# Top-k attention with a capacity-limited expert layer: the order of one maximum, one pick and one mask in every second step

## The chip, the cores and the metric

The kernel runs on one core of a Trainium2 chip. A core has five engines that run side by side, each with its own stream of instructions, and wait for one another through semaphores: TensorE (PE in the profile, with its weight loads as PEld), VectorE (DVE), ScalarE (ACT), GpSimd (POOL) and SyncE (SP), which here only issues transfers. The metric is the device time of one execution in microseconds (us).

## What is computed

Two blocks follow each other. The first is attention over 8 batches, 8 heads, 576 positions and 64 features, in which each row keeps its 32 largest scores and drops the others:

```python
scores = scale * np.matmul(q, k.transpose(0, 1, 3, 2))
kth = np.partition(scores, -top_k, axis=-1)[..., -top_k:-top_k + 1]
mask = scores >= kth
scores = np.where(mask, scores, -1000000000.0)
...
attn = np.exp(scores)
attn = attn / (np.sum(attn, axis=-1, keepdims=True) + 1e-09)
return np.matmul(attn, v).astype(np.float32)
```

The second takes the 4608 x 512 result as tokens, sends each to the best of 8 experts, keeps the 80 tokens with the largest gate per expert, and runs two matrix products with a ReLU between them on those:

```python
logits = x @ w_gate
expert_idx = np.argmax(logits, axis=1)
...
h = np.maximum(x[tok_idx] @ w1[e], 0.0)
out[tok_idx] = gate_w[tok_idx, None] * (h @ w2[e])
```

All of the change lies in the first block: in how the 32nd largest score of each row is found, and in the mask that is made from it.

## The kernel before

The work is cut into 288 **units**. Two heads make a head pair; there are 32 head pairs, n = 0 to 31. A head pair has four full row tiles of 128 rows with two heads each, which are eight units, and one last tile in which the remaining 64 rows of both heads stand below one another, which is the ninth unit. So unit u = 9n + o, with o = 0 to 8, and a unit is a matrix `s` of 128 rows and 576 scores.

The threshold of a unit is found in this way (`search`, cuts marked). The eight largest of each of six parts (`parts`, not shown) are candidates; three rounds of maximum and replacement on the 48 candidates give the 24th largest of these, `w9[:, 7]`. ScalarE counts, with a sign function, how many scores lie above it. A product of the scores with that sign turns the larger ones negative, so that the maximum over the product gives the next eight scores below. The pick then takes from those nine values the one that the count calls for: the 32nd largest.

```python
def search(self, i):
    ...
            nc.scalar.activation(sign, s, Act.Sign, bias=w9[:, 7:8], scale=-1.0, accum_out=cnt)      # L266
    ...
    y = self.rows.tile([P, S], F32, name="y", tag="y", bufs=1)
    engine = nc.gpsimd if i in self.odd else nc.vector
    engine.tensor_tensor(out=y, in0=s, in1=sign, op=Alu.mult)                                        # L273, the product
    yield
    nc.vector.max(out=w9[:, 8:], in_=y)                                                              # L275, the maximum
    yield
    pick = self.small.tile([P, TOP_K - G0 + 1], F32, name="pick", tag="pick")
    nc.vector.scalar_tensor_tensor(out=pick, in0=past, scalar=cnt, in1=w9[:, 7:], accum_out=self.thr[:, i : i + 1],
                                   op0=Alu.is_equal, op1=Alu.mult)                                   # L278, the pick
    yield
```

The product of an odd unit is made by GpSimd, that of an even one by VectorE; there is one buffer `y` for both. The mask of dropped scores is made the other way round, by ScalarE for odd units and by GpSimd for even ones:

```python
def below(self, i):
    self.top.pop(i)
    mask = self.mask_of(i)
    if i in self.odd:
        nc.scalar.activation(mask, self.s[i], Act.Relu, bias=self.thr[:, i : i + 1], scale=-1.0)     # L294
        return
    nc.gpsimd.tensor_scalar(mask, self.s[i], self.thr[:, i : i + 1], None, op0=Alu.is_lt)            # L296
```

TensorE transposes the scores of a tile into PSUM (L334), adds the mask times a huge negative number (L340), ScalarE takes the exponential (L343 and L344), and TensorE multiplies by `v` (L357). A tile has one or two units, and its mask product in TensorE's stream comes behind the masks of both.

The units are pipelined by hand. A loop over steps emits, in step i, pieces of the units i to i - 4. The letters of a string give the order: each stands for one piece, and `lag` says of which unit.

```python
lag = dict(a=0, b=1, c=1, d=1, e=1, y=2, g=3, h=4, m=4)

for c in "ghmGbGycGdGGGeaz" if i % 2 else "GbGhmgcGdGeGGyaz":
    if c == "G":
        if 0 <= i < NU:
            next(first[i])                 # one of the six parts' maxima, L250
    elif c == "a":
        ...                                # the last part, then the first round on the candidates, L261
    elif c == "z":
        for u in drawn:
            self.over(*u)                  # reciprocal of the row sums, L369
    elif c == "m":
        if 0 <= i - lag[c] < NU:
            self.below(i - lag[c])         # the mask
    elif i - lag[c] in second:
        next(second[i - lag[c]])           # b, c, d, e: rounds; y: product; g: maximum; h: pick
...
if whole(i - 4):
    self.turn_w(*units[i - 4][:2], gate)   # transposes, mask products, exponentials of the tile
...
```

So in an even step, `y` is VectorE's product of unit i - 2, `g` is the maximum over GpSimd's product of the odd unit i - 3 (issued to GpSimd in the step before), `h` is the pick of the even unit i - 4, and `m` is GpSimd's mask of that unit. Instructions run on each engine in the order in which they are emitted.

Of the kernel before, what the change touches and what calls it, by code (L numbers as in the profile page):

```python
# [27 lines left out]
def kernel(  # L28
# [120 lines left out]
    class Attention:  # L149
# [299 lines left out]
        def run(self, slow):  # L449
# [13 lines left out]
            def whole(i):  # L463

                return 0 <= i < NU and units[i][2] > 0

            def step(i, last):
                if 0 <= i < NU:
                    n, t, h = units[i]
                    if t == 2 and h == 1 and n + 2 < NP:  # L470
                        self.load(n + 2, *divmod(n + 2, HP))
                    if t == 3 and h == 1 and n + 2 < NP:
                        self.load_v(n + 2, *divmod(n + 2, HP))
                    if t in (1, 3) and h == 0 and slow and n:
                        slow.pop(0)()
                    if t == 0 and h == 0 and n + 1 < NP:
                        due.append(n + 1)
                    first[i] = self.parts(i)

                lag = dict(a=0, b=1, c=1, d=1, e=1, y=2, g=3, h=4, m=4)  # L480

                for c in "ghmGbGycGdGGGeaz" if i % 2 else "GbGhmgcGdGeGGyaz":
                    if c == "G":
                        if 0 <= i < NU:
                            next(first[i])
                    elif c == "a":
                        if 0 <= i < NU:
                            next(first[i], None)
                            second[i] = self.search(i)
                            next(second[i])  # L490
                    elif c == "z":
                        for u in drawn:
                            self.over(*u)
                    elif c == "m":
                        if 0 <= i - lag[c] < NU:
                            self.below(i - lag[c])
                    elif i - lag[c] in second:
                        next(second[i - lag[c]])
                done = list(drawn)
                drawn.clear()  # L500

                def back():
                    if whole(i - 5):
                        self.back(*units[i - 5][:2])
                        drawn.append(units[i - 5][:2])


                rest = whole(i - 4) and units[i - 4][2] == 2
                if rest:
                    back()  # L510
                def gate():
                    for g in later:
                        if ready[g] == 2:
                            ready[g] = next(g)

                if whole(i - 4):
                    self.turn_w(*units[i - 4][:2], gate)
                for u in done:
                    self.divide(*u)

                ends = [(n, range(NK) if n < NP - 1 else range(NF) if t < NF else range(NF, NK))
                        for n, t in done if t == NF or (n == NP - 1 and t == NF - 1)]

                f = i + 4 if i not in (0, 1) else i + 3
                busy = 0 <= f < NU and units[f][2] != 1
                if busy:
                    self.front(*units[f][:2])
                if not rest:
                    back()
                if due and not busy and i > 0:  # L530
                    self.turn(due.pop())
                    busy = True
                for g in list(later):
                    if (ready[g] == 1 and busy or ready[g] == 2 and i < NU + 4) and not last:
                        continue
                    busy = busy or ready[g] == 1
                    ready[g] = next(g, None)
                    if ready[g] is None:
                        later.remove(g)
                for n, cs in ends:  # L540
                    b, hp = divmod(n, HP)
                    later.append(self.norm(n, b, hp, b % 2, 2, cs))
                    ready[later[-1]] = 0

            with tc.manual_schedule():
                for n in range(2):
                    self.load(n, *divmod(n, HP))
                    self.load_v(n, *divmod(n, HP))
                nc.sync.dma_start(wg, moe_w_gate.rearrange("(c p) e -> p c e", p=P))
                self.turn(0)  # L550
                i = -4
                while i < NU + 6 or later:
                    step(i, i >= NU + 5)
                    i += 1
# [391 lines left out]
```

## Time and profile before

| | |
|---|---|
| time, median of 3 runs | 989.52 us (988.08 to 991.57) |
| profiled execution | span 986.1 us, 35265 instructions |
| DVE, chain that ended last | 59% of the span |
| PE, chain that ended last | 29% of the span |
| the maximum (L275), 288 times | 752 ns each on DVE |
| the pick (L278), 288 times | 230 ns each on DVE |
| the product (L273), 144 times each | 740 ns on DVE, 1281 ns on GpSimd |
| the mask, 144 times each | 785 ns on ACT (L294), 1722 ns on GpSimd (L296) |
| the sign (L266), 288 times | 781 ns each on ACT |

The attention loop takes most of the span, from about 12 us to about 850 us; then routing and the experts follow. A line of the profile's timeline gives start and duration in us, the engine, the line of the kernel, the operation, what is written from what is read, the shapes, and in brackets how long the engine was idle just before it and what ended that. VectorE's instructions overlap a little at their ends: the time from one start to the next is shorter than the duration that is shown. An instruction with an accumulated output (the sign, the pick) is followed by a short read of the accumulator, and only then is its result there.

### The profile page before, as it was taken

To read this page: it belongs to the slowest core of one execution; us is meant where nothing else is said; L and a number is where in the kernel's file an instruction comes from. 1 tells how busy PE (TensorE), PEld (TensorE's weight loads), DVE (VectorE), ACT (ScalarE), POOL (GpSimd) and SP (SyncE) were. 2 spreads that over 40 slices of the span, in tenths; PEclk is the share of its full clock that TensorE was granted. 3 is DMA by queue.
4 is the path that set the end of the run, shared out by engine and by line. 5 is a ranking of instruction groups with operands and counts; after the bars stand their busy time and mean duration, and the time that the engine had idled before them with its cause. 6 is when DMAs were issued, how large, how long until landed. Compare 5 with 4: busy or idle time off the path is not lost.

```text
span 986.1 us, 35265 instructions
## 1 busy us (share of the span) xinstructions
PE 865.1 (88%) x13112; PEld 679.3 (69%) x13112; DVE 866.3 (88%) x5072; ACT 786.7 (80%) x1652; POOL 451.9 (46%) x333
## 2 busy tenths in 40 slices
PE   5898989898898998998889898988898898699896
PEld 3676767676666776776667676666676776578896
DVE  5999999999999999999999999999999999561110
ACT  4899999999899999999999999998999998501110
POOL 2455545555455555454555555554555555201111
PEclk9999999999999999999999999999999999979999
DMA  3445453333333333332221222222222200085910
GB/s 86 111 131 139 133 141 100 100 99 99 80 95 99 88 93 99 99 99 68 57 57 48 52 50 53 57 57 57 57 57 56 55 17 14 17 338 180 375 52 25
DMA packets 189812, 90.99 MB, mean 92 GB/s; under 512 B 139712, under 2 KB 176576, under 8 KB 189632
## 3 DMA queue, kind: packets, MB, share of 16 engines
q1 hardware_dynamic: 188608, 86.03, 31.5%
q0 software_dynamic: 1024, 2.62, 0.9%
q8 instruction: 105, 1.72, 0.7%
q14 instruction: 75, 0.61, 0.2%
HBM read 68.44 MB, written 20.19 MB: 90 GB/s over the span
## 4 chain that ended last, share of the span: by engine, by line
DVE 59%; PE 29%; ACT 7%; issue 3%; POOL 1%; DMA 1%; SPq 0%; POOLq 0%; ACTq 0%; DVEq 0%
DVE cand L250 19%; DVE w L275 14%; DVE cand L269 7%; DVE y L273 7%; PE cc L357 6%; PE sp L234 4%; DVE top L261 4%; PE yp L830 4%; PE sp L209 4%; DVE pick L278 3%; DVE w L261 2%; PE ab L334 2%; ACT wT L344 2%; ACT mask L294 1%; PE ab L340 1%
## 5 line engine op out<-in xcount | busy, mean ns | idle before, releaser
L250 DVE MAX8 cand<-s 128x8 f32<-128x96 f32 x1728 | 389.6, 246 | 9.1 <-ACT s L242 8.9
L296 POOL TENSOR_SCALAR mask<-s,thr_all 128x576 bf16<-128x576 f32 x144 | 247.9, 1722 | 149.6 <-DVE pick L278 130.1
L273 POOL TENSOR_TENSOR y<-s,sign 128x576 f32<-128x576 f32 x144 | 184.5, 1281 | 261.8 <-DVE pick L278 121.9
L266 ACT ACTIVATE sign<-s,w 128x576 bf16<-128x576 f32 x288 | 224.9, 781 | 29.6 <-DVE w L261 27.3
L357 PEld LDWEIGHTS cc<-vb,wT 128*64 128x64 f32 x5760 | 182.1, 138 | 92.0 <-ACT wT L344 90.7
L357 PE MATMUL cc<-vb,wT 128*64 128x65 f32 x5760 | 204.4, 225 | 25.7 <-ACT wT L344 25.7
L275 DVE MAX8 w<-y 128x8 f32<-128x576 f32 x288 | 216.6, 752 | 1.3 <-POOL y L273 1.3
L234 PE MATMUL sp<-both 64*128 64x288 f32 (+1 forms) x1280 | 202.0, 435 | 5.7 <-ACT s L242 3.8
L242 ACT ACTIVATE s<-sp 128x1152 f32<-128x1152 f32 (+1 forms) x161 | 167.6, 1042 | 10.5 <-PE sp L234 9.8
L334 PE MATMUL ab<-ident,s 128*128 128x128 f32 x1148 | 175.9, 281 | 0.0
L344 ACT ACTIVATE wT<-ab 128x1024 f32<-128x1024 f32 (+1 forms) x159 | 149.6, 941 | 5.6 <-PE ab L340 4.1
L234 PEld LDWEIGHTS sp<-both 64*128 64x128 f32 (+1 forms) x1280 | 105.5, 179 | 45.2 <-ACT s L242 6.2
L334 PEld LDWEIGHTS ab<-ident,s 128*128 128x128 f32 x1148 | 127.2, 141 | 11.7 <-issue 0.9
L340 PEld LDWEIGHTS <-mask 128*128 128x128 bf16 x1312 | 76.9, 97 | 79.1 <-issue 37.3
L261 DVE MAX8 top<-cand 128x8 f32<-128x48 f32 x576 | 115.2, 200 | 0.0
L294 ACT ACTIVATE mask<-s,thr_all 128x576 bf16<-128x576 f32 x144 | 113.0, 785 | 0.5
L269 DVE MATCH_REPLACE8 cand<-top,cand 128x48 f32<-128x48 f32 x576 | 111.0, 193 | 0.1
L273 DVE TENSOR_TENSOR y<-s,sign 128x576 f32<-128x576 f32 x144 | 106.6, 740 | 0.8 <-ACT sign L266 0.8
L340 PE MATMUL ab<-huge,mask 128*128 128x128 bf16 x1148 | 89.9, 219 | 0.0
L340 PE MATMUL cc<-huge,mask 128*128 128x128 bf16 x160 | 35.7, 223 | 58.9 <-ACT mask L294 29.0
L380 ACT ACTIVATE xn<-cc,z_all 128x64 f32<-128x64 f32 (+1 forms) x320 | 85.8, 315 | 1.2 <-DVE z_all L369 0.8
L278 DVE SCALAR_TENSOR_TENSOR pick<-past,cnt,w 128x9 f32<-128x9 f32 x288 | 66.4, 230 | 0.2 <-DVE z_all L369 0.2
(187 smaller groups left out, 856.0 us busy)
## 6 DMA issues: line engine op xcount, KB each, us to landing
w<-in_moe_w_dram SPq DMA_DIRECT2D x10, 2048.0 KB, 16.0
vb<-in_v_dram SPq DMA_DIRECT2D x96, 128.0 KB, 2.7
w<-in_moe_w_dram SPq DMA_DIRECT2D x24, 512.0 KB, 3.8
out_dram<-zero SPq DMA_DIRECT2D x9, 1024.0 KB, 5.8
qn<-in_q_dram SPq DMA_DIRECT2D x64, 128.0 KB, 2.3
kn<-in_k_dram SPq DMA_DIRECT2D x64, 128.0 KB, 2.6
xd<-xn SPq DMA_DIRECT2D x32, 256.0 KB, 2.2
qn<-in_q_dram SPq DMA_DIRECT2D x32, 32.0 KB, 2.5
```

Source lines behind the costliest of these rows:

```text
L234: nc.tensor.matmul(o, lhsT=qT[d, t * P : t * P + m], rhs=kT[d, j * HS : (j + 1) * HS], start=True, stop=True)
L250: nc.vector.max(out=cand[:, j, :], in_=s[:, j * S // NG : (j + 1) * S // NG])
L261: nc.vector.max(out=dst, in_=cand)
L266: nc.scalar.activation(sign, s, Act.Sign, bias=w9[:, 7:8], scale=-1.0, accum_out=cnt)
L269: nc.vector.match_replace(out=cand, in_to_replace=dst, in_values=cand, imm_value=LOW)
L273: engine.tensor_tensor(out=y, in0=s, in1=sign, op=Alu.mult)
L275: nc.vector.max(out=w9[:, 8:], in_=y)
L296: nc.gpsimd.tensor_scalar(mask, self.s[i], self.thr[:, i : i + 1], None, op0=Alu.is_lt)
L334: nc.tensor.matmul(o, lhsT=sc[:, keys[c]], rhs=ident, start=c in (0, NF, NF + 1), stop=False, is_transpose=True, skip_group_check=True)
L340: nc.tensor.matmul(dst[c], lhsT=mk[:, keys[c]], rhs=minus if self.lean else huge, start=False, stop=True, skip_group_check=True)
L344: nc.scalar.activation(wT[:, : g * NF, :], ab.rearrange("p h c r -> p (h c) r")[:, : g * NF, :], Act.Exp, scale=scale / TINY)
L357: nc.tensor.matmul(cc[r : r + TL, o], lhsT=wT[:, h * NF + c if c < NF else 2 * NF, r : r + TL], rhs=vb[:, k, :], start=(c == 0), stop=(c = ...
```

## The change

In even steps the maximum over GpSimd's product (`g`) is emitted ahead of the pick (`h`) and of GpSimd's mask (`m`). Odd steps stay as they are; there the maximum has always come first.

```diff
                 lag = dict(a=0, b=1, c=1, d=1, e=1, y=2, g=3, h=4, m=4)

-                for c in "ghmGbGycGdGGGeaz" if i % 2 else "GbGhmgcGdGeGGyaz":
+                for c in "ghmGbGycGdGGGeaz" if i % 2 else "GbGghmcGdGeGGyaz":
                     if c == "G":
                         if 0 <= i < NU:
                             next(first[i])
```

On VectorE each of the 144 even steps then has "maximum of unit i - 3, pick of unit i - 4" where it had "pick, maximum"; the two do not depend on each other. The streams of the other four engines keep their order. The aim is to have the maximum done earlier and so its one product buffer free earlier; GpSimd's mask of the even unit, which needs the pick, then comes behind the maximum.

## The prediction

> **What bounds the kernel now.** I read the page's first two parts, then busy times by stage, the waits, and the instructions in order of time over two head pairs.
>
> ```profile
> PE 865.1 (88%) x13112; PEld 679.3 (69%) x13112; DVE 866.3 (88%) x5072; ACT 786.7 (80%) x1652; POOL 451.9 (46%) x333
> ```
>
> That is the page's first part, busy time by engine. By stage (stretch, length, then PE, PEld, DVE, ACT, POOL busy):
>
> ```profile
> 200.00:400.00 200.00, 178.29 (x2564) 137.03 (x2564) 199.62 (x1200) 185.63 (x390) 104.14 (x70) 1.00 0.36 95
> 400.00:600.00 200.00, 180.30 (x2616) 138.97 (x2613) 199.68 (x1197) 185.84 (x390) 103.79 (x70) 1.00 0.26 66
> ```
>
> PE and DVE look alike over the whole span, but in the attention loop DVE works 199.6 of 200 us; what DVE lacks is in the start and in the expert tail. So an instruction moved on DVE saves nothing unless a wait goes with it, and every new wait of DVE adds to the time. ACT (93% in the loop) and PE (89%) have little room.
>
> DVE shows one hidden wait. A pick takes 0.21 us as a rule, yet:
>
> ```profile
> 311.10 1.28 POOL L273 TENSOR_TENSOR y<-s,sign 128x576 f32<-128x576 f32 x1 [2.78 <-ACT sign L266]
> ...
> 311.89 0.51 DVE L278 SCALAR_TENSOR_TENSOR pick<-past,cnt,w 128x9 f32<-128x9 f32 x1
> ...
> 312.41 0.76 DVE L275 MAX8 w<-y 128x8 f32<-128x576 f32 x1
> ...
> 312.58 1.72 POOL L296 TENSOR_SCALAR mask<-s,thr_all 128x576 bf16<-128x576 f32 x1 [0.20 <-DVE pick L278]
> ```
>
> GpSimd's product ends at 312.38; the pick is drawn out to that moment and the maximum starts at 312.41. This recurs once in two head pairs (12 times at this place, and three times at the ends of the loop). In all other even steps the product is done 0.47 to 1.3 us before its maximum, so bringing the maximum forward by one pick needs no wait there.
>
> **What the mask releases.** The even steps also make GpSimd's mask. Number the units u = 9n + o (n the head pair, 0 to 31). For odd n an even unit is the second head of its tile, and PE folds the mask in within the same step; for even n it is the first head, and PE needs it a step later (for the single last tile, the same step, but 2.49 us after the mask is done). In odd n:
>
> ```profile
> 317.94 0.21 DVE L278 SCALAR_TENSOR_TENSOR pick<-past,cnt,w 128x9 f32<-128x9 f32 x1
> ...
> 318.08 0.75 DVE L275 MAX8 w<-y 128x8 f32<-128x576 f32 x1
> 318.33 1.72 POOL L296 TENSOR_SCALAR mask<-s,thr_all 128x576 bf16<-128x576 f32 x1 [1.19 <-DVE pick L278]
> ...
> 319.79 0.74 DVE L273 TENSOR_TENSOR y<-s,sign 128x576 f32<-128x576 f32 x1
> ...
> 320.11 0.23 PE L340 MATMUL cc<-huge,mask 128*128 128x128 bf16 x1 [1.44 <-POOL mask L296]
> ```
>
> Pick, mask (ends 320.05), PE: PE has already stood 1.44 us. From there ACT and PE run in turn up to 335.78 without waiting once more for DVE or GpSimd: ACT's idle times are 0.15, 0.17 and 0.32 us, all for PE, and PE waits only for ACT. At the end of that run stands a sign which DVE's own product reads:
>
> ```profile
> 388.43 0.23 ACT L266 ACTIVATION_READ_ACCUMULATOR sign<-s,w 128x1 f32 x1
> ...
> 388.76 0.74 DVE L273 TENSOR_TENSOR y<-s,sign 128x576 f32<-128x576 f32 x1
> ```
>
> The sign is ready at 388.66, its product starts at 388.76: a margin of 0.10 us (0.20 us at 336.68, a head-pair couple earlier; the two alternate). The closest that any product follows its sign in the trace is 0.03 us, so the real slack is 0.07 or 0.17 us.
>
> [...] the long picks show time that belongs to a wait as busy; DVE's 199.6 of 200 us thus holds about 0.3 us of waiting per two head pairs. [...] DVE's product starts at 319.79, 0.26 us before the mask ends, and neither 0.74 nor 1.72 us grows. [...]
>
> **The change part by part.** Nothing is removed or added; the orders of PE, ACT, GpSimd and SyncE stay. On DVE, in all 144 even steps, maximum (u+1) and pick (u) swap. Slots, start to start: the maximum 0.66 us (318.08 to 318.75 is 0.67), the pick 0.14 us (317.94 to 318.08).
> - DVE's sum of work: unchanged, 0.
> - The pick's completion, and so GpSimd's mask: later by 0.67 us.
> - Where the product is late (15 places) the maximum still starts at the product's end, but the pick, which ran inside the wait, now comes behind: +0.14 us on DVE.
> - Even n: PE has 2.5 us in hand or takes the mask a step later; 0.
> - Odd n, the step of 318: the mask is later by 0.67 + 0.14 = 0.81 us, PE likewise (it waited already), and the ACT and PE run carries all 0.81 to the sign at its end. The masks after it have 0.25 to 0.42 us of slack to PE and then come after 0.81 us of PE's own delay, so they add nothing. DVE itself is late by the 0.14, so it waits 0.67 - slack, and ends the head pair late by 0.81 less 0.07 or 0.17: 0.74 or 0.64 us.
> - Then even n: ACT waits for DVE's candidates twice there (0.54 us at 340.24, 0.81 at 346.21), so what ACT is late beyond DVE (0.07 to 0.17) vanishes, and the next two head pairs start afresh. What DVE has lost stays lost.
>
> The sum over the 15 places where an odd n passes into an even one: 15 x 0.81 = 12.15; for n = 9, 17, 25 there was no late product: minus 3 x 0.14 = 0.42; minus slacks 8 x 0.07 + 7 x 0.17 = 1.75; gives 10.0. The three late products at the ends of the loop add 3 x 0.14 = 0.4. 989.5 + 10.4 = 999.9 us, or 1.05% slower.
>
> **Rivals.**
> 1. *Nothing moves* (989 to 991). For it: DVE has the same work, and an earlier maximum frees the one y buffer earlier. Against: that buffer's next writer is DVE itself, later in the same step in the same order, so nothing can start earlier; and PE's 1.44 us wait shows that the mask is wanted at once.
> 2. *The full delay accumulates* (about 1003): 15 x 0.81 + 0.4 = 12.6 with no slack eaten, or the late ACT reaches the next late product of GpSimd before the even head pair has absorbed it. Against: the two idle times of ACT there.
> 3. *PE or ACT becomes the bound* (1005 and more): PE waits 0.67 us longer in each of 4 steps of 16 odd head pairs, 43 us if all of it counted. Against: only the first or second of each row waits; later ones are behind PE's own work.
> 4. [...] a mask 0.67 us later lies under nearly all of DVE's product (319.0 to 320.7 against 319.79 to 320.5). Were they exclusive, each of 144 products would wait about 0.9 us, 130 us in all. Against: the overlap of 0.26 us that costs nothing now.
> 5. *Faster*: the pick is no longer held under GpSimd's product. Against: the maximum then waits for the same end of the same product.
>
> **Range and chances.** Rivals 1 and 2 lie near 990 and 1003; the slack that I take as 0.07 and 0.17 may be off by 0.1 in 15 places (1.5 us), and the runs of before spread over 3.5 us. I predict 999.9 us, 8 in 10 between 994 and 1004. Slower by over 2% (above 1009.3) needs rival 3 or 4: 0.03. Faster by over 2% needs 20 us from an engine whose work is unchanged: 0.005.
>
> **What would show it.** DVE's list of waits should gain its product (line 273) waiting for ACT's sign, about 15 times and some 0.5 us each, early in even head pairs; picks of even steps should all be 0.21 us, and the maximum waits for GpSimd's product visibly, 0.3 to 0.5 us about 15 times. PE's wait for GpSimd's mask should grow from 1.44 to about 2.1 us in the second tile of odd n. The length of two head pairs (51.6 us) should grow by 0.6 to 0.75 us. If PE's waits grow and DVE's do not, the slack behind the mask was larger than I read it; [...] if the growth is 0.81 us or more, the delay was not absorbed.

## The result and the profile after

The changed kernel takes 1002.08 us (median of 4 runs, 1001.68 to 1003.38) against 990.02 us for the kernel before beside it. The ratio is 1.0125, with a 95% interval of 1.0104 to 1.0146: 12.1 us slower.

The first two fences are from the page of the changed kernel: busy time by engine, and the shares by engine in the chain of work that ended last.

```profile
PE 868.6 (87%) x13112; PEld 680.0 (68%) x13112; DVE 864.8 (86%) x5072; ACT 790.2 (79%) x1652; POOL 451.8 (45%) x333
```

```profile
DVE 43%; PE 29%; ACT 16%; POOL 6%; issue 4%; DMA 1%; SPq 0%; POOLq 0%; ACTq 0%; DVEq 0%
```

No engine has more instructions; DVE's share of the chain fell from 59% to 43%, and ACT (from 7%) and GpSimd (from 1%) took its place. By stage, with the columns as before (stretch, length, then PE, PEld, DVE, ACT, POOL busy):

```profile
200.00:400.00 200.00, 177.57 (x2545) 136.02 (x2543) 196.46 (x1177) 183.31 (x384) 102.03 (x68) 1.00 0.35 93
400.00:600.00 200.00, 176.78 (x2566) 135.61 (x2563) 197.17 (x1184) 183.53 (x382) 102.28 (x69) 1.00 0.26 65
```

DVE now works 196.5 to 197.2 of 200 us, where it worked 199.6. Of its list of waits over the whole kernel (who waited for whom: us in total, times, longest), two lines have grown from 1.3 and 0.8 us, each then seen once or twice:

```profile
DVE w L275 <- POOL y L273: 9.3, 16, 1.5
...
DVE y L273 <- ACT sign L266: 7.6, 29, 0.4
```

And this is the stretch that the prediction rests on, now five microseconds later, from the timelines of DVE, GpSimd, ACT and PE (start, duration, engine, line, operation, idle time ahead and what ended it). First the place where GpSimd's product is late:

```profile
316.08 1.28 POOL L273 TENSOR_TENSOR y<-s,sign 128x576 f32<-128x576 f32 x1 [2.13 <-ACT sign L266]
...
317.40 0.76 DVE L275 MAX8 w<-y 128x8 f32<-128x576 f32 x1 [0.45 <-POOL y L273]
318.07 0.21 DVE L278 SCALAR_TENSOR_TENSOR pick<-past,cnt,w 128x9 f32<-128x9 f32 x1
```

Then the mask that this pick releases, and ACT behind it:

```profile
318.46 1.72 POOL L296 TENSOR_SCALAR mask<-s,thr_all 128x576 bf16<-128x576 f32 x1 [1.10 <-DVE top L261]
...
320.24 0.23 PE L340 MATMUL cc<-huge,mask 128*128 128x128 bf16 x1 [0.72 <-POOL mask L296]
...
320.51 0.28 ACT L343 ACTIVATE wT<-cc 128x128 f32<-128x128 f32 x1 [0.52 <-PE cc L340]
320.95 1.02 ACT L344 ACTIVATE wT<-ab 128x1024 f32<-128x1024 f32 x1 [0.17 <-PE ab L340]
...
325.24 0.76 DVE L273 TENSOR_TENSOR y<-s,sign 128x576 f32<-128x576 f32 x1 [0.24 <-ACT sign L266]
...
325.91 0.23 PE L340 MATMUL cc<-huge,mask 128*128 128x128 bf16 x1 [1.35 <-POOL mask L296]
...
342.65 0.76 DVE L273 TENSOR_TENSOR y<-s,sign 128x576 f32<-128x576 f32 x1 [0.21 <-ACT sign L266]
```

In the kernel before, PE and ACT stood in the same place as follows, without a wait:

```profile
314.37 0.22 PE L340 MATMUL cc<-huge,mask 128*128 128x128 bf16 x1
...
314.89 0.28 ACT L343 ACTIVATE wT<-cc 128x128 f32<-128x128 f32 x1
...
315.07 1.02 ACT L344 ACTIVATE wT<-ab 128x1024 f32<-128x1024 f32 x1
```

The reader is to see the whole chain in it. The maximum waits for the product (317.40) and the pick stands behind it. The mask starts 5.88 us later than before (318.46 and 312.58) where the product starts 4.98 us later (316.08 and 311.10): it is 0.90 us late against its surroundings. PE waits for it (0.72 us where it did not wait at all), ACT waits for PE (0.52 and 0.17 us), and one sign later VectorE waits for ACT: at 325.24, where the read of that sign's accumulator ends at 325.21, and again at 342.65. An idle time is shorter than the delay that it makes: most VectorE instructions of this trace that follow one another without a wait overlap by 0.08 to 0.09 us, and each of the 29 products that waited takes 0.76 us, where the others take 0.74 (median). So 0.24 us of idleness is 0.34 us lost, 0.21 us is 0.31.

In what follows, "lost in a stretch" is how much later a maximum of the same unit starts in the timeline than in the kernel before, taken at both ends of the stretch. From one odd head pair to the next (18 units, 51.6 us) the change loses about 0.8 us (0.79 to 0.83) and about 0.9 us (0.91 to 0.93) in turn; three of the fifteen stretches, those that begin with head pairs 9, 17 and 25, lose 0.61 or 0.62 us. The fifteen sum to 12.1 us.

### The profile page after: what moved, and what is told of

The parts are those of the page before. It is cut to its first block, busy times and chain, and to the rows that moved or that the text cites. A ratio compares the mean times of both kernels' runs of the same rounds, so it can differ in the third digit from the quotient of the medians.

```text
span 1001.6 us, 35265 instructions
## 1 busy us (share of the span) xinstructions
PE 868.6 (87%) x13112; PEld 680.0 (68%) x13112; DVE 864.8 (86%) x5072; ACT 790.2 (79%) x1652; POOL 451.8 (45%) x333
## 4 chain that ended last, share of the span: by engine, by line
DVE 43%; PE 29%; ACT 16%; POOL 6%; issue 4%; DMA 1%; SPq 0%; POOLq 0%; ACTq 0%; DVEq 0%
DVE cand L250 12%; DVE w L275 10%; PE cc L357 6%; DVE y L273 6%; PE sp L209 5%; ACT sign L266 5%; DVE cand L269 5%; POOL y L273 4%; PE sp L234 4%; PE yp L830 4%; ACT s L242 4%; DVE top L261 3%; ACT wT L344 3%; ACT mask L294 2%; DVE pick L278 2%
## 5 line engine op out<-in xcount | busy, mean ns | idle before, releaser
L278 DVE SCALAR_TENSOR_TENSOR pick<-past,cnt,w 128x9 f32<-128x9 f32 x288 | 61.2, 213 | 0.2 <-DVE z_all L369 0.2
```

## The experiments

Each kernel is the one before with one line edited, unless more is shown. An even step is named by the unit whose pick it makes, u = 9n + o. Times are medians beside runs of the kernel before on the same chip; a ratio has its own comparison of runs and is not exactly the quotient of the two medians.

| run | time, us | before, us | ratio (95%) |
|---|---|---|---|
| swap_o1 | 995.98 | 988.88 | 1.0075 (1.0052 to 1.0098) |
| swap_o3 | 1006.43 | 988.88 | 1.0166 (1.0142 to 1.0190) |
| swap_o5 | 995.95 | 988.88 | 1.0066 (1.0045 to 1.0087) |
| swap_o7 | 989.91 | 988.88 | 1.0013 (1.0003 to 1.0024) |
| swap_even | 990.74 | 989.89 | 1.0005 (0.9995 to 1.0014) |
| swap_odd | 1002.94 | 989.89 | 1.0127 (1.0107 to 1.0148) |
| late_max | 989.41 | 989.89 | 0.9995 (0.9985 to 1.0005) |
| first_pick | 995.38 | 989.89 | 1.0048 (1.0032 to 1.0064) |
| o3_filled | 998.45 | 989.21 | 1.0096 (1.0080 to 1.0112) |
| late_pick | 987.20 | 989.21 | 0.9973 (0.9964 to 0.9982) |

### The swap in one of the four steps of an odd head pair

```diff
-"ghmGbGycGdGGGeaz" if i % 2 else "GbGhmgcGdGeGGyaz":
+"ghmGbGycGdGGGeaz" if i % 2 else "GbGghmcGdGeGGyaz" if (i - 4) % 18 == 10 else "GbGhmgcGdGeGGyaz":
```

That is o = 1; 12, 14 and 16 in place of 10 give o = 3, 5 and 7.

> The maximum goes ahead of the pick only in the step of unit o = 1 of odd head pairs (16 of 144 even steps), where GpSimd's product comes late. Chain theory (mask to PE to ACT to sign to VectorE's product): 0.14 us for the pick that now stands behind the wait, and a mask that is 0.88 us later reaches the sign of the next tile as 0.90 us, against 0.43 us of slack and 0.14 us of VectorE's own delay: 0.34 us of waiting. 0.48 us in 12 places, about 0.2 us in the three head pairs (9, 17, 25) without a late product: +6.4 us. Rival, every swap costs the same 12.1 / 144 = 0.084 us on VectorE: +1.3 us. Rival, what counts is PE's added wait: 16 x 0.88 = +14 us.

Measured: +7.1 us. A stretch between two odd head pairs loses 0.49 to 0.53 us where the product is late: 0.15 us at the pick and 0.35 at VectorE's product of unit o = 5. Of the three others, two lose more than expected, 1.05 and 0.47 us (head pairs 9 and 17); both have what the next run shows, a halving of PE's clock (mean granted clock of the profiled run 0.984, 0.986 to 0.988 in those of the kernel before beside it). The third loses 0.07 us. The chain theory stands. The rival of PE's added wait is out: PE's idle time ahead of its mask products into `cc` sums to 59.0 us over the kernel, against 58.9 us before, and yet the run is 7 us longer.

> The swap only in the step of unit o = 3 of odd head pairs. Chain theory: the mask is 0.67 us later, PE was already waiting 1.44 us for it, ACT and PE carry 0.67 us to the sign read early in the next head pair, with 0.07 or 0.17 us of slack: 8 x 0.60 + 7 x 0.50 = +8.3 us; all of it as VectorE's product waiting for the sign at unit o = 3 of even head pairs. Rival, equal cost per swap: +1.3 us. Rival, PE's added wait: 16 x 0.67 = +10.7 us.

Measured: +17.5 us by the medians (single runs 1004.06 to 1011.66, of which the longest was profiled), more than the whole change, which has this swap among others. The expectation was far off. Yet six of the fifteen stretches lose what was expected, 0.49 to 0.61 us; nine lose 1.9 to 2.1 us. What these nine have in common stands in the busy times by stage, with PE's granted clock as the third number from the right:

```profile
324.02:327.43 3.41, 1.32 (x17) 0.98 (x15) 3.41 (x18) 2.44 (x6) 1.72 (x1) 1.00 0.56 126
327.43:330.84 3.41, 3.41 (x32) 2.38 (x34) 3.41 (x27) 2.54 (x5) 2.14 (x2) 0.50 0.46 163
330.84:334.25 3.41, 3.41 (x60) 2.92 (x57) 2.61 (x14) 2.93 (x8) 1.04 (x2) 1.00 0.02 5
```

PE waits 2.1 us for the mask, is busy for 1.32 of 3.41 us, and in the next 3.41 us has half its clock (0.50). In the same run's timeline of PE:

```profile
326.75 0.23 PE L340 MATMUL cc<-huge,mask 128*128 128x128 bf16 x1 [2.09 <-POOL mask L296]
...
327.36 2.26 PE L234 MATMUL sp<-both 64*128 64x288 f32 x8
329.54 1.97 PE L357 MATMUL cc<-vb,wT 128*64 128x65 f32 x40
```

Those eight score matmuls take 1.24 us and those forty 1.39 us elsewhere. PE comes a further 1.6 us late, and VectorE's product waits twice for a sign that comes in time where the clock is whole:

```profile
332.32 0.76 DVE L273 TENSOR_TENSOR y<-s,sign 128x576 f32<-128x576 f32 x1 [0.80 <-ACT sign L266]
...
338.67 0.76 DVE L273 TENSOR_TENSOR y<-s,sign 128x576 f32<-128x576 f32 x1 [0.48 <-ACT sign L266]
```

One halving thus costs about 1.4 us, some 1.95 less 0.5 or 0.6. The mean granted clock of the four runs goes the same way: 0.978 in the run of 1004.06 us, 0.976 in those of 1006.33 and 1006.53 us, 0.971 in that of 1011.66 us; the runs of the kernel before have 0.986 to 0.990. The changed kernel has no halving ahead of its last head pair: its granted clock is 1.00 from 31.30 to 860.68. (Halvings are counted up to there: the kernel before has one in its last head pair, at 835.31, and the changed kernel one at 860.68, each of 3.41 us at 0.50.)

> The swap only in the step of unit o = 5 of odd head pairs. Chain theory: of the mask's 0.67 us, 0.25 us are slack to PE (it turns the queries of an output row block first), 0.42 us go on to the sign with 0.07 or 0.17 us of slack: 8 x 0.35 + 7 x 0.25 = +4.6 us. Rival, equal cost per swap: +1.3 us.

Measured: +7.1 us by the medians, 5.9 us at the end of the loop in the trace; a stretch loses 0.41 to 0.44 or 0.30 to 0.33 us, some 0.07 us more than expected. The sign at the end of the run comes 0.47 us late in the trace, so the mask's slack was about 0.20 us and not 0.25. No halving (mean granted clock 0.987). The chain theory stands, with this term mis-sized.

> The swap only in the step of unit o = 7 of odd head pairs. Chain theory: the mask has 0.31 to 0.42 us of slack to PE, and ACT then takes its exponential 0.85 us after PE's first mask product where 0.31 us would do, because it is busy with a sign: together more than the 0.67 us. +0 us, within 1. Rival, equal cost per swap: +1.3 us. Rival, PE's added wait counts: 16 x 0.3 = +5 us.

Measured: +1.0 us, and in the trace no stretch loses more than 0.01 us, although PE waits 0.12 to 0.25 us for this mask where it did not wait before. So equal cost per swap is out, as the four sites cost 7, 17, 7 and 0 to 1 us, and PE's added wait by itself costs nothing here.

### Even and odd head pairs apart

```diff
+... "GbGghmcGdGeGGyaz" if (i - 4) // 9 % 2 == 0 else "GbGhmgcGdGeGGyaz":     # swap_even
+... "GbGghmcGdGeGGyaz" if (i - 4) // 9 % 2 else "GbGhmgcGdGeGGyaz":          # swap_odd
```

> The swap in all even steps of even head pairs (80 of the 144), none in odd ones. Chain theory: there GpSimd's mask is wanted a step later or 2.49 us after it is done, so its 0.67 us go nowhere; only two late products at the start of the loop cost 0.14 us each: +0.3 us, within 1. Rival, every swap costs the same: 80 x 0.084 = +6.7 us. Rival, PE loses clock wherever the mask is late: some us more.

Measured: +0.05%, no difference; no stretch loses more than 0.04 us. The 80 swaps of the even head pairs are free.

> The swap in all even steps of odd head pairs (64 of 144). Chain theory: the whole of the change's cost, +12 us, and less than the swap at o = 3 alone, because a late mask at o = 1 makes PE come late to the mask at o = 3, so that PE's idle time is split into two shorter ones and its clock is not halved. Rival, the clock depends on chance alone: several halvings of 3.4 us in the loop and +18 us. Rival, every swap costs the same: +5.4 us.

Measured: +13.1 us, all of the change. Stretches lose 0.8 or 0.9 us as in the full change; one loses 1.70 us, and in it lies the only halving ahead of the last head pair, against nine in swap_o3 (mean granted clocks of the two profiled runs 0.986 and 0.971). The four swaps together cost 13 us, where the four alone sum to 33 us. In the changed kernel PE's idle time is in two pieces, 0.72 us (320.24) and 1.35 us (325.91), where swap_o3 has one of 2.09 us.

### Is it the clock?

swap_o3 again, with work for PE where it would stand still. The product of zeros goes to columns of a tile that nobody reads.

```diff
+[nc.tensor.matmul(cc[:, 3 * P :], lhsT=zero, rhs=zero, start=False, stop=True, skip_group_check=True)
+ for _ in range(8 if n % 2 and t == 1 and not self.lean else 0)]
 for c in sorted(range(len(dst)), key=lambda c: c != NF):                      # the mask products
```

> The swap at o = 3 of odd head pairs alone, as before, and ahead of the mask products of that tile eight matmuls of zeros on zeros, which add nothing to columns that nobody reads; PE would stand there for some 2.1 us otherwise. Theory: what that swap cost beyond the chain's 8.3 us came from halvings of PE's clock, [...] no halving in the loop, +0.50 or +0.60 us in every two head pairs, +8.3 us in all. Rival, the halvings have another cause, or more work on PE only delays the mask products: +16 us or more.

Measured: +9.2 us, against +17.5 us without the filling, at a mean granted clock of 0.988 in all four runs. From the timeline of PE:

```profile
321.36 1.95 PE L338 MATMUL cc<-zero 128*128 128x128 f32 x16
323.62 0.23 PE L340 MATMUL cc<-huge,mask 128*128 128x128 bf16 x1 [0.31 <-POOL mask L296]
...
324.22 1.24 PE L234 MATMUL sp<-both 64*128 64x288 f32 x8
```

PE has 1.95 us more to do, waits 0.31 us, and is back at 1.24 us for the score matmuls. No halving is left ahead of the last head pair, and every stretch loses 0.52 to 0.65 us. So what swap_o3 cost beyond the chain was the halved clock, shown by filling the idle time and leaving the late mask as it was.

### The other direction: a later maximum, an earlier pick

```diff
-"GbGhmgcGdGeGGyaz"
+"GbGhmcGdGegGGyaz"    # late_max
+"hmGbGgcGdGeGGyaz"    # first_pick
```

> The other way round: in even steps the pick and the mask stay where they were before the change, and the maximum over GpSimd's product goes behind the third round on the candidates, about 1.3 us later. Chain theory: the mask is as before, the 15 hidden waits for a late product (4.6 us in all by the long picks) vanish, and ScalarE's sign of the odd unit starts 0.66 us earlier: -4 us, with VectorE idle nowhere in the loop. Rival, the waits only move to VectorE's product or to the masks: 0.

Measured: no difference; the expectation failed. The long picks are still there, though no maximum stands behind them any more. From the timelines of DVE and GpSimd of late_max:

```profile
312.30 0.53 DVE L278 SCALAR_TENSOR_TENSOR pick<-past,cnt,w 128x9 f32<-128x9 f32 x1
...
312.75 0.20 DVE L261 MAX8 top<-cand 128x8 f32<-128x48 f32 x1
```

```profile
311.52 1.27 POOL L273 TENSOR_TENSOR y<-s,sign 128x576 f32<-128x576 f32 x1 [2.79 <-ACT sign L266]
```

GpSimd's product ends at 312.79 and the pick at 312.83, with an instruction behind it that waits for nothing of GpSimd.

> In even steps the pick and the mask come at the very start of the step, 0.7 us earlier than before the change; the maximum stays. Chain theory: VectorE has no wait that the earlier mask could take away, so PE's wait for the mask shrinks from 1.44 to about 0.75 us and the time stays: 0, within 1 us. Rival, the delay works both ways and the earlier mask gains what the later one cost: -12 us.

Measured: +5.5 us by the medians, +0.48%; the expectation failed here too. The trace gives 0.40 to 0.46 us more in each of the twelve stretches with a late product, and nothing in the rest:

```profile
313.70 1.28 POOL L273 TENSOR_TENSOR y<-s,sign 128x576 f32<-128x576 f32 x1 [3.29 <-ACT sign L266]
...
313.97 1.03 DVE L278 SCALAR_TENSOR_TENSOR pick<-past,cnt,w 128x9 f32<-128x9 f32 x1
```

The pick comes earlier within the product and is held longer, 1.03 us, up to the product's end at 314.98. So the pick itself is held. In the kernel before, too, the picks that start under a product of GpSimd are the fifteen long ones, and each ends 0.03 us behind the end of that product. The maxima and replacements that VectorE runs beside the same product in the kernel before (311.20 to 311.89) keep their usual length, 0.19 to 0.25 us. Nor does a mask of GpSimd hold VectorE's product: in the changed kernel the mask runs from 324.13 to 325.85, and the product that starts under it at 325.24 takes 0.76 us. Of the 143 products of VectorE that start under such a mask in that kernel, 142 take 0.73 to 0.76 us, and the mask never takes more than 1.74 us. By what the pick is held is not shown; no run gave the pick or GpSimd's product another form.

### The pick where the product has ended

If the pick is held, it can be put later at no cost, but only where the product is late:

```diff
-"ghmGbGycGdGGGeaz" if i % 2 else "GbGhmgcGdGeGGyaz":
+"ghmGbGycGdGGGeaz" if i % 2 else "GbGcGhmgdGeGGyaz" if (i - 4) % 18 == 10 else "GbGhmgcGdGeGGyaz":
```

> Only in the step of unit o = 1 of odd head pairs, where GpSimd's product comes late: pick, mask and maximum go one round on the candidates and one part's maximum later (about 0.3 us). Theory: the long pick is not VectorE waiting for its next instruction but the pick itself, [...] held by GpSimd's product until that ends; doing two one-input instructions first uses that time, the pick still ends when the product does, and the mask starts within 0.1 us of where it did: 12 x 0.28 = -3.4 us (-0.3%). Rival, the pick is not held and its end moves by 0.3 us, so the mask does too: +1 to +3 us.

Measured: -2.0 us by the medians, ratio 0.9973 (0.9964 to 0.9982): faster than both kernels, by little. The trace has 0.23 to 0.26 us less in each of the twelve stretches, 3.0 us in all. From the timelines of DVE and GpSimd of this run:

```profile
311.11 0.27 DVE L278 SCALAR_TENSOR_TENSOR pick<-past,cnt,w 128x9 f32<-128x9 f32 x1
```

```profile
310.08 1.28 POOL L273 TENSOR_TENSOR y<-s,sign 128x576 f32<-128x576 f32 x1 [2.80 <-ACT sign L266]
311.56 1.72 POOL L296 TENSOR_SCALAR mask<-s,thr_all 128x576 bf16<-128x576 f32 x1 [0.20 <-DVE pick L278]
```

The pick still ends with the product (311.36), now after 0.27 us in place of 0.51, and the mask starts 1.48 us after the product does, as before (312.58 less 311.10). VectorE did two other instructions in the time.

## Why the prediction was right, and where it was not

The measured 1002.08 us lies within the range of 994 to 1004; 10.4 us slower was predicted, 12.1 measured.

- *VectorE has no more work; only new waits count.* Right: its busy time is 864.8 us, 1.5 less than before, and it works 196.5 or 197.2 of 200 us.
- *Even head pairs lose nothing.* Right, by swap_even.
- *The late mask reaches a sign through PE and ACT in odd ones.* Right, by the wait at 342.65 and by swap_odd. The wait at 325.24 comes in the same way, from a mask that the prediction did not follow (below); so VectorE's list has 29 such waits where about 15 were predicted.
- *At the step of 318, PE takes the mask 0.81 us later.* Right: 325.91 is 0.82 us behind 320.11, after the 4.98 us by which everything is later when that head pair starts.
- *ACT catches up in the even head pair, so that each two head pairs start afresh.* Right: ACT still waits for VectorE's candidates there, 0.40 us in place of 0.54 (at 346.04). The second rival, whose 12.6 us are near the result, has the wrong cause. A growth of 0.81 us or more per two head pairs was named as the sign that the delay is not absorbed; stretches lose 0.79 to 0.93 us although it is absorbed, so this sign misleads.
- *The masks after it add nothing, and VectorE is late only by the 0.14 us of the pick.* This is the step that was wrong, by a term left out. The prediction follows the mask of the step of 318 and those after it; from the place of the late product, one tile earlier, it takes the pick's 0.14 us and not the mask. That mask has its own way to a sign. In the kernel before, ACT came to its first exponential 0.52 us after PE's first mask product began, and the rest was then nearly done; but once ACT waits for PE's first mask product, it also waits for the other eight before the second exponential: 0.44 us from one start to the next (320.51 to 320.95), where it was 0.18 (314.89 to 315.07). The whole 0.90 us reach the sign, 0.34 us of it VectorE's product. VectorE is then late by 0.48 us and not 0.14, and the mask of o = 5, later by 0.48 + 0.67 with about 0.20 us of slack, overtakes the 0.81 us: the sign at the end of the run is 0.96 us late. Less its slack, a stretch loses about 0.8 or 0.9 us where 0.64 or 0.74 were predicted. Twelve stretches by some 0.17 us are the 2.1 us between 10.0 predicted and 12.1 found in the fifteen stretches. The three without a late product lose 0.61 or 0.62 us; 0.60 was predicted. swap_o1 has this term alone: 0.35 us.
- *The long pick is a wait shown as busy.* Wrong: the pick is held by GpSimd's product, not by the wait of the maximum (0.53 us in late_max with no maximum behind it, 1.03 us in first_pick). For the change this made no difference, as the maximum waits for the same end: 0.45 us at 317.40, and no pick longer than 0.22 us is left between 15 and 840 us.
- *A later mask and VectorE's product do not shut each other out (fourth rival).* Right, by the 142 of 143 products above.
- *PE's wait for the second tile's mask grows to 2.1 us.* Not in the changed kernel, where it is 1.35 us, because PE comes 0.9 us late from the tile before. Alone, in swap_o3, it is 2.09 us.
- *The PE bound (third rival).* Not in the change. But the prediction did not see that PE's idle time can cost clock; in swap_o3 it did (mean granted clock 0.971 to 0.978).

What stays open: that GpSimd's product is late at that one place because its sign stands behind the copy at L222 in ScalarE's stream was only read from the trace, and not tried. What tells a stretch of PE with a halving behind it from one without is not shown (see the last section). The medians differ by 12.1 us and the loops of the two profiled runs by 13.2; the tail behind the loop was not looked into.

## What to carry to other kernels

When an engine is full, moving two of its independent instructions past each other saves nothing there, unless one of them stands waiting or held (late_pick); ask instead which of the two another engine is waiting for, and do not put the other ahead of it. Putting it earlier still cost 5.5 us here, because it was held (first_pick). A delay must be followed along each of its ways, and a wait at one instruction can bring a second with it when the producer delivers in parts (0.52 and 0.17 us of ACT for PE at 320.51 and 320.95). A busy instruction that is longer than its fellows is worth a look: put something else in its place, and see whether it still ends with the other engine's instruction.

## What was not expected of the hardware

- PE's clock was halved (0.50) for 3.41 us after stretches of 3.41 us in which PE was busy for about a third to a half: 1.32 us (39%) ahead of the halving at 327.43 in swap_o3, 1.31 us (38%) ahead of the one at 542.47, and 1.69 us (50%) ahead of the one at 835.31 in the kernel before. In swap_o1, swap_o3 and swap_odd twelve such halvings lie ahead of the last head pair, each right behind a stretch with PE busy for 33 to 51% (the shares are by the matmul spans of the trace). In the changed kernel the granted clock goes between 1.00 and 0.50 at 860.68, 864.09, 874.33, 884.57, 898.23 and 905.05: 3.41, 10.24, 10.24, 13.65 and 6.83 us apart, which is 1, 3, 3, 4 and 2 times 3.413. The busy share does not tell which stretch has a halving behind it. In the kernel before, one with 1.76 of 3.40 us (52%) had none:

```profile
473.50:476.90 3.40, 1.76 (x32) 1.46 (x28) 3.40 (x22) 2.86 (x5) 2.14 (x2) 1.00 0.52 119
476.90:480.30 3.40, 3.36 (x59) 2.62 (x60) 3.40 (x23) 3.25 (x8) 1.29 (x1) 1.00 0.12 25
```

  Nor had one with 1.64 of 3.41 us (48%) in swap_o3:

```profile
57.80:61.21 3.41, 1.64 (x27) 1.33 (x23) 3.41 (x21) 3.07 (x6) 1.56 (x2) 1.00 0.55 126
61.21:64.62 3.41, 3.09 (x57) 2.44 (x57) 3.41 (x26) 2.72 (x7) 1.55 (x2) 1.00 0.60 163
```

  At the end of the changed kernel's attention loop, on the other hand, a stretch with PE busy for 1.81 us (53%, from 857.27) was followed by a halving.

  So a wait of 2.1 us in swap_o3 cost about 1.4 us through the clock in nine stretches, beside 0.5 or 0.6 us through its own delay, and only the latter in the other six. One of these six has a wait of 2.10 us too, which ends at 434.23, and no halving follows. If stretches of 3.413 us are counted on from the halving at 327.43 (the one at 542.47 is 63 of them later), a boundary falls into this wait, at 433.24 (31 later), and cuts it in two; that this is why no halving follows is an estimate from these times. That the single runs of swap_o3 spread over 7.6 us, with the clocks given above, fits such an effect of where the waits fall.
- A pick of 0.21 us took 1.03 us under GpSimd's product in first_pick, while 142 of the 143 products of VectorE that start under GpSimd's mask in the changed kernel took 0.73 to 0.76 us. What makes the difference was not separated.
